# A long-convolution layer and a Mish MLP on one core: a reordered schedule, D's transfer first, and other V chunks

## The chip, the cores and the metric

The kernel runs on one core of a Trainium2 chip. A core has a matrix engine (TensorE, PE in the profile), which multiplies into PSUM, and four other engines: VectorE (DVE), ScalarE (ACT), GpSimd (POOL) and SyncE (SP), which here only issues DMAs. Each engine works through its own queue in order; semaphores tie them together. The metric is the device time of one execution in microseconds (us); lower is better.

## The reference

Two blocks, with a residual around each, on S = 2048 positions of D = 640 channels; the MLP has F = 1728 hidden units.

```python
def _A_ref(q, k, v, shift_k, ssm_k, ssm_D):
    k_shift = jnp.zeros_like(k)
    for t in range(4):                                   # short causal convolution of k
        k_shift = k_shift + k_pad[:, t:t + S, :] * shift_k[:, 3 - t][None, None, :]
    kv = k_shift * v
    y = irfft(rfft(kv, 2 * S) * rfft(ssm_k, 2 * S))[:S]  # long causal convolution, per channel
    y = y + kv * ssm_D[None, None, :]
    return q * y

def _B_ref(x, w1, b1, w2):
    h = einsum("bsd,df->bsf", x, w1) + b1
    act = h * tanh(softplus(h))                          # Mish
    return einsum("bsf,fd->bsd", act, w2)

x = A_q
h = x + _A_ref(_layernorm(x), A_k, A_v, A_shift_k, A_ssm_k, A_ssm_D)
return h + _B_ref(_layernorm(h), B_w1, B_b1, B_w2)
```

All inputs and the output are bfloat16.

## The kernel before

*The work.* The long convolution is a transform in two stages of matmuls, applied to the filter ("k" in the names) and to the product kv ("v"), a multiplication in the transformed domain, and two inverse stages. Channels come in five blocks of 128 (dc 0 to 4). Steps are tokens with a name, a block and a piece:

- `d_n0`..`d_n4` load the filter, 512 KB a block; `d_k0`..`3`, `d_v0`..`3`, `d_x0`..`3` load k, v and x (640 KB each), `d_g0`..`7` the table of the second stage (512 KB each), `d_cst` and `d_t2m`, `d_a12` other tables, `d_dr` the vector D, `d_w1*`, `d_w2*` the MLP's weights.
- D is folded into the filter: `dsel`, `dcol` (lines 273, 274) arrange it as a column for each block, and `dadd*` (line 364) adds it to the filter's first column. `k1pe*` transposes a filter block (line 370), and `k1ev*` (line 375) copies it out of PSUM. Block 0 is copied in two halves, `k1ev0` and `k1ev0b`.
- `s1kpe`, `s1kev`: first stage of the filter, 20 groups (lines 390, 391) and their copies; `s2kpe`, `s2kev`: second stage, 22 groups (line 416). A copy is line 256 on ACT and line 258 on DVE.
- `ktpe`, `ktev`, `ktsh`: k transposed (line 335), copied, shifted. `coef`, `wsh` (lines 303, 311) make the matrices of the short convolution; `kspe` (lines 351, 352) applies it and `kv` (line 356) multiplies with v on DVE.
- `s1v*`, `s2v*`: the two stages of kv. The second stage runs in chunks of channel blocks, `CHUNKS`; a group of a chunk may start when the first stage of all its blocks is copied out. `s2v0`, `s2v1`, `s2v2` are the chunks in their order.
- `sw*` (line 444): ten DMAs, two for each block, that swap the halves of the filter's transform within SBUF; `pr*` (line 455): 20 products on DVE; `i1pe`, `i1ev` (line 473): inverse first stage; `i2*`, `y` (line 525): inverse second stage and its copies.
- The first layer norm: `ln1_` (DVE statistics, lines 504, 505), `ln1p` (POOL, lines 509 to 511), `lnx` (ACT line 516 or POOL line 518). Then `wb`, `h` (lines 532, 534), the second norm `bn`, `pow`, `hc` (lines 538 to 544), and a transposition of each of 16 tiles of rows: the first two by PE (`trpe`, `trev`), the others by DMA (`tr`, line 557).
- The MLP: `m1pe` (lines 582, 589) with its activations `hb` (ACT, line 604), `m2pe` (lines 647, 655), `res` (line 672) and `d_out`. Rows come in units of 256, 256, 512, 512, 512.

*The order.* One list, `ORDER`, written out by hand, holds all 660 steps. The steps are emitted in this order, so each engine's queue is the list cut down to its own steps. `@n` names the PSUM tile that a PE group writes; there are four tiles, of two banks each, and a group waits until the earlier contents of its tile are copied out. `:a`, `:d`, `:p` pick ACT, DVE or POOL for a step that may run on more than one; without it the step runs on the first engine of its list. A DMA on SP's or ACT's queue takes one of eight semaphores in turn, and SP waits until the DMA eight places earlier has landed before it issues the next.

*Around the change.* ACT's queue begins with three DMAs, `d_cst`, `d_dr`, `d_sk`. SP's begins `d_n0 d_n1 d_n3 d_n4 d_k2 d_a12 d_k0 d_n2 d_k3 d_k1`. `dadd1` and `dadd2` run on DVE, the other three on POOL. The last steps before the MLP's matmuls are `wb0 h0 wb1 h1 bn0 bn1 wb3 hc0 h3 hc1` on DVE, and eleven `y` copies, `trev0` and `trev1` on ACT.

Of the kernel before, what the change touches and what calls it, by code (L numbers as in the profile page):

```python
# [30 lines left out]
s1kev2_1 ktpe1_3 ktpe4_0@2 wsh3 d_g0 ktev1 ktpe4_2 ktpe0_0@1 ktpe4_1 ktpe4_3 ktpe2_0@0 ktev4 ktpe3_0@3 ktpe2_2 ktpe3_3 d_g4 ktpe3_2 ktpe3_1 ktpe2_1
ktev3 s1kpe1_1@2 ktpe2_3 s1kev1_1 ktpe0_3 ktev2 ktpe0_1 ktsh3 d_g5 ktpe0_2 s1kpe3_0@3 ktsh1 s1kpe2_0@2 ktev0 ktsh4 s1kev3_0 kspe4_1@0 d_g3 ktsh2
s1kev2_0 ktsh0 kspe3_0@3 kv4_1 s1kpe2_3@1 s1kpe4_2@2 kv3_0 s1kev2_3 s1kpe4_0@0 s1kev4_2 s1kpe2_2@1 s1kev4_0:d kspe4_0@3 s1kev2_2 kspe0_0@2 kv4_0
s2kpe_96@0 s2kpe_30@1 kv0_0 s2kev_96 kspe1_0@3 s2kev_30 s2kpe_42@0 kv1_0 s2kpe_24@2 s2kev_42 kspe2_0@1 s2kev_24:d s2kpe_120@3 s2kpe_108@0 s2kev_120
kv2_0 kspe1_1@2 s2kev_108 s2kpe_12@3 kv1_1 d_x0 s2kpe_36@1 s2kev_12 d_x1 kspe0_1@0 s2kev_36:d s2kpe_90@2 s2kpe_48@3 s2kev_90 kv0_1 kspe2_1@1 s2kev_48
s2kpe_78@2 kv2_1 s1vpe4_1@0 s2kev_78 s2kpe_6@3 s1vev4_1 s2kpe_66@1 ln1_1 s2kpe_84@2 s2kev_66 kspe3_1@0 s2kev_84:d ln1p1 s2kev_6 s2kpe_0@1 kv3_1
s2kpe_60@2 s2kev_0 s1vpe2_0@3 s2kev_60 d_x2 s1vpe2_2@0 s1vev2_0:d s1vpe2_1@1 d_x3 s1vev2_2 s1vpe0_1@2 lnx1:p s1vev2_1:d s2kpe_102@3 s1vev0_1
s2kpe_72@0 s2kev_102:d s1vpe1_0@1 s2kev_72 s1vpe3_0@2 s1vev1_0 s1vpe0_2@3 s1vev3_0:d s1vpe1_3@0 s1vev0_2 s2kpe_126@1 ln1_0 s2kpe_114@2 s2kev_126
s1vpe2_3@3 s1vev1_3 s2kev_114:d s2kpe_54@1 ln1p0 s1vev2_3 s2kpe_18@0 s2kev_54:d s1vpe0_0@2 s2kev_18 s1vpe4_0@3 ln1_3 s1vpe3_2@1 s1vev0_0 sw2_1
s1vpe4_2@0 sw1_0 s1vev3_2:d s1vev4_0 ln1p3 s1vpe1_2@2 sw1_1 s1vev1_2 sw3_1 s1vpe1_1@3 s1vev4_2:d lnx3:p s1vpe3_3@1 sw4_1 s1vev1_1 s1vpe0_3@2  # L40
s1vev3_3:d lnx0:p sw3_0 s1vpe4_3@0 s1vev0_3 sw0_0 s1vpe3_1@3 ln1_2 sw2_0 s2v1pe_112@1 s1vev4_3 s2v1pe_96@2 sw0_1 s1vev3_1:d s2v1ev_112 ln1p2 sw4_0
s2v1pe_48@0 d_t2m s2v1ev_48 s2v1ev_96:d s2v1pe_32@1 lnx2:p s2v1pe_64@3 s2v1ev_32 s2v2pe_80@0 pr1_96 b1pe@2 s2v1ev_64 s2v1pe_80@1 pr1_32 s2v2ev_80
s2v1pe_0@3 s2v1ev_80:d s2v1ev_0 s2v1pe_16@0 s2v1ev_16 s2v2pe_32@3 pr1_64 s2v2pe_0@1 c_b1 s2v2ev_32 s2v2pe_48@0 pr1_0 s2v2pe_64@2 s2v2ev_48 pr2_64
i1pe1_0@3 s2v2ev_0 s2v2pe_112@0 pr2_96 s2v2ev_64 i1pe1_1@1 i1ev1_0 pr4_32 s2v2pe_16@2 s2v2ev_112 i1pe1_2@3 pr2_0 s2v2ev_16 pr2_32 s2v2pe_96@0 i1ev1_1
s2v0pe_0@2 pr3_0 i1ev1_2 i1pe2_3@1 s2v0ev_0 pr3_32 s2v0pe_64@3 s2v2ev_96 i1pe2_0@2 pr3_64 s2v0ev_64 s2v0pe_96@0 pr3_96 i1ev2_3 s2v0pe_32@3 pr4_0
i1ev2_0 i1pe2_1@1 d_w10 d_w11 s2v0ev_96 i1pe3_1@2 pr4_64 d_w12 i1ev2_1 d_w14 i1pe3_2@0 pr0_0 d_w13 s2v0ev_32 i1pe3_3@1 pr4_96 i1ev3_2 i1pe3_0@3
i1ev3_3 pr0_32 i1pe4_2@0 i1ev3_0 i1pe4_1@1 pr0_96 i1ev3_1 i1pe1_3@3 ln1_6 i1ev4_2 i1pe4_3@2 pr0_64 ln1p6 i1ev1_3 i1pe2_2@0 i1ev4_1 ln1_5 i1pe0_0@3
lnx6:p i1ev2_2 i1pe0_2@1 ln1_9 ln1p5 i1ev0_0 i1pe0_1@0 ln1_4 lnx5:p i1ev0_2 i1pe0_3@3 i1ev0_1:d ln1p4 i1ev4_3 i1pe4_0@1 ln1_7 i1ev0_3 ln1p9 d_w2b
i1ev4_0 d_w2c ln1_11 i2a1@0 d_w2a ln1p7 i2a0@2 i2b0 ln1_14 i2b1 i2pe9@3 y0 i2pe4@1 y1 wb0 i2a3@2 y9 h0 i2pe11@0 wb1 y4 i2b3 h1 i2a2@3 y11 bn0 i2b2
i2pe10@1 y2 i2pe5@0 y10 bn1 i2pe7@3 pow0 y3 i2pe6@1 y7 i2pe12@2 wb3 pow1 y6 hc0 h3 trpe0@3 y12 i2pe13@1 hc1 trev0:a wb2 trpe1@2 bn3 trev1:a i2pe8@3  # L50
y13 m1pe0_4@2 h2 pow3 y8 bn2 lnx9 ln1p11 m1pe0_2@1 hc3 y5 m1pe0_6@3 wb6 tr3 pow2 hb0_2 wb5 m1pe0_1@0 w2z lnx7 hc2 ln1_10 tr2 m1pe0_3@1 hb0_4 lnx11:p
hb0_6 h5 m1pe0_0@2 ln1p14 lnx4 ln1_15 hb0_3 m1pe0_5@3 h6 hb0_0 bn6 m1pe1_5@1 hb0_1 wb7 lnx14 pow6 m1pe1_4@2 bn5 ln1p15 hb1_5 m1pe1_1@0 hb1_4 hc6 h7
tr6 pow5 hb0_5 m1pe1_2@1 bn7 ln1p10 hb1_1 m1pe1_0@2 hc5 ln1_12 pow7 tr5 m1pe1_6@3 hb1_0 hc7 ln1p12 hb1_2 ln1_8 tr7 m1pe1_3@0 hb1_6 wb11 i2pe14@2 h11
hb1_3 wb4 i2pe15@1 wb9 lnx10 m2pe0@3 h4 h9 y14 bn4 lnx12 ln1_13 pow4 ln1p8 hc4 m2pe2@0 wb10 tr4 h10 ln1p13 lnx8 bn11 lnx15 bn10 pow11 y15 lnx13 wb8
pow10 hc11 m1pe2_3@2 res2 wb12 d_out2 h12 tr11 h8 m1pe2_2@1 wb14 res0 bn8 d_out0 m2pe1@0 bn9 pow8 wb13 pow9 hc8 hc10 wb15 tr10 h13 h14 m1pe2_4@3 hb2_3
hc9 tr8 bn13 hb2_2 tr9 h15 pow13 m1pe2_5@2 bn12 bn14 pow12 m1pe2_6@1 hb2_5 hc13 bn15 tr13 hb2_4 m2pe3@2 hc12 pow15 hb2_6 tr12 pow14 hc15 hc14 tr14
tr15 m1pe3_1@3 res3 res1 d_out3 d_out1 m1pe3_6@1 hb3_1 m1pe3_0@2 hb3_6 m1pe3_2@0 hb3_0 m1pe3_4@3 hb3_2 m1pe2_1@1 hb3_4 m1pe3_5@2 hb2_1 m1pe2_0@0 hb3_5
m1pe3_3@3 hb2_0 m2pe4@1 hb3_3 m2pe6@2 m2pe5@0 res6 res4 d_out6 d_out4 m2pe7@3 m1pe4_3@2 res7 res5 d_out5 d_out7 m1pe4_5@1 hb4_3 m1pe4_2@3 hb4_5
# [108 lines left out]
def kernel(  # L167
# [193 lines left out]

    k1_pes, k1_evs = [], []
    for b in range(NDC):
        dad = OP(f"dadd{b}", ["dve", "pool"], [d_n[b], o_dc], emit=lambda e, b=b: (nc.gpsimd if e == "pool" else nc.vector).tensor_tensor(raw_n[b][:, 0:1], raw_n[b][:, 0:1], dcol[:, b:b + 1], ALU.add))
# [12 lines left out]


# [339 lines left out]
```

## Time and profile before

| | us |
|---|---|
| median of 3 runs (228.49 to 228.54) | 228.52 |
| profiled execution, device time | 227.92 |
| its span, first to last instruction | 226.1 |
| PE busy in the span | 215.3 (95%) |
| DVE busy | 140.7 (62%) |
| ACT busy | 131.4 (58%) |
| POOL busy | 52.4 (23%) |

The profile records one execution. Times in it count from the first instruction. L364 is line 364 of the kernel. Busy time of PE includes waiting in its pipeline; a number in square brackets is the idle time of the engine ahead of an instruction, with what ended it. Shares over the whole span mix two very different halves, so the views below are cut into stretches. TensorE's clock was granted in full (1.00) throughout.

### The profile page before, as it was taken

Reading aid. Unit: us, or ns where it says so; the run is one execution under the profiler, and the core shown is the slowest. Engines: PE = TensorE matmul, PEld = TensorE weight load, DVE = VectorE, ACT = ScalarE, POOL = GpSimd, SP = SyncE. Lnnn points to the kernel's source line nnn. Section 1 sums busy time; section 2 is a strip of 40 time slices with the busy share of each in tenths; the row PEclk is TensorE's granted clock in tenths of the full one; section 3 lists DMA queues with packets and bytes.
Section 4 is the critical chain, followed back from the end, with each engine's and each line's share of the span. In section 5 each row is a group of like instructions: output and inputs, shape, how many; then the busy total and the mean of one; then the engine's idle time right before and its main releaser. Section 6 shows DMA issues by size and latency. Waiting matters only on the chain.

```text
span 226.1 us, 6202 instructions
## 1 busy us (share of the span) xinstructions
PE 215.3 (95%) x2690; PEld 157.5 (70%) x2690; DVE 140.7 (62%) x250; ACT 131.4 (58%) x181; POOL 52.4 (23%) x101
## 2 busy tenths in 40 slices
PE   7999999999979999999999999999999999999994
...
GB/s 206 371 421 415 418 343 33 210 232 97 414 412 206 167 259 4 185 192 33 29 77 38 62 58 89 137 12 3 0 0 58 29 32 0 3 29 46 58 53 48
DMA packets 19563, 30.98 MB, mean 137 GB/s; under 512 B 10704, under 2 KB 14928, under 8 KB 18768
## 3 DMA queue, kind: packets, MB, share of 16 engines
...
q14 instruction: 6, 0.05, 0.1%
...
HBM read 20.42 MB, written 2.62 MB: 102 GB/s over the span
## 4 chain that ended last, share of the span: by engine, by line
PE 67%; DMA 9%; DVE 9%; ACT 7%; SPq 3%; issue 3%; POOL 1%; DVEq 0%; ACTq 0%
PE ps L647 25%; PE ps L582 25%; DMA ks<-in_A_ssm_k_dram 6%; DVE ks L455 5%; PE ps L473 3%; ACT uv L256 3%; ACT ks L256 3%; SPq L444 3%; DMA ks<-ks 3%; PE ps L335 2%; PE ps L416 2%; PE ps L351 2%; PE ps L390 2%; PE ps L352 1%; PE ps L589 1%
## 5 line engine op out<-in xcount | busy, mean ns | idle before, releaser
L604 ACT ACTIVATE ks<-ps,b1s 128x512 bf16<-128x512 f32 (+1 forms) x69 | 36.2, 617 | 44.0 <-PE ps L582 35.8
L647 PE MATMUL ps<-ks 128*128 128x320 bf16 (+2 forms) x420 | 58.6, 299 | 0.0
L582 PE MATMUL ps<-G 128*128 128x512 bf16 (+1 forms) x325 | 57.6, 337 | 0.1
L672 DVE TENSOR_TENSOR rb<-ps,rb 128x640 bf16<-128x640 f32 x15 | 11.8, 820 | 68.4 <-PE ps L655 66.0
L647 PEld LDWEIGHTS <-ks 128*128 128x128 bf16 x420 | 40.6, 98 | 17.3 <-issue 1.3
L582 PEld LDWEIGHTS <-G 128*128 128x128 bf16 x325 | 31.3, 98 | 24.7 <-issue 1.6
L256 ACT CAST uv<-ps 128x1024 bf16<-128x1024 f32 x50 | 46.6, 1145 | 0.0
L256 ACT CAST ks<-ps 128x640 bf16<-128x640 f32 (+3 forms) x46 | 37.9, 898 | 10.1 <-PE ps L391 6.7
L455 DVE TENSOR_TENSOR ks<-ks,uv 128x2048 bf16<-128x2048 bf16 x20 | 23.0, 1221 | 0.8 <-DMA ks<-ks 0.6
L416 PEld LDWEIGHTS <-G 128*128 128x128 bf16 x512 | 20.9, 96 | 3.1 <-issue 2.5
L473 PE MATMUL ps<-a_t,ks 128*128 128x128 bf16 x320 | 19.2, 219 | 1.3 <-DVE ks L455 1.2
L473 PEld LDWEIGHTS <-ks 128*128 128x128 bf16 x320 | 18.2, 113 | 1.8 <-DVE ks L455 1.6
L509 POOL TENSOR_SCALAR ve<-mv 128x1 f32<-128x1 f32 x16 | 4.7, 294 | 48.2 <-DVE mv L505 47.3
L542 POOL TENSOR_TENSOR r<-ve,mhalf 128x1 f32<-128x1 f32 x16 | 10.2, 638 | 21.7 <-DVE ve L540 21.7
L416 PE MATMUL ps<-uv,G 128*128 128x64 bf16 (+1 forms) x384 | 12.9, 187 | 1.7 <-ACT uv L256 1.4
L538 DVE BATCH_NORM_STATS2 st<-rb 128x6 f32<-128x320 bf16 x32 | 14.1, 482 | 0.1
L258 DVE CAST ks<-ps 128x1024 bf16<-128x1024 f32 (+1 forms) x12 | 14.0, 1179 | 0.2
L504 DVE BATCH_NORM_STATS2 st<-rb 128x6 f32<-128x320 bf16 x32 | 13.9, 475 | 0.0
L356 DVE TENSOR_TENSOR ra<-ps,rb 128x1024 bf16<-128x1024 f32 x10 | 11.9, 1219 | 1.1 <-PE ps L352 0.7
L258 DVE CAST uv<-ps 128x1024 bf16<-128x1024 f32 x10 | 11.9, 1211 | 0.5 <-PE ps L391 0.2
L390 PE MATMUL ps<-cst,ks 128*64 128x128 bf16 x160 | 10.8, 220 | 0.9 <-DVE ks L258 0.5
L390 PE MATMUL ps<-cst,ra 128*64 128x128 bf16 x160 | 10.5, 219 | 0.8 <-ACT uv L256 0.5
...
## 6 DMA issues: line engine op xcount, KB each, us to landing
...
G<-tab_g SPq DMA_DIRECT2D x8, 512.0 KB, 11.4
...
```

The costliest lines, as they stand in the source:

```text
L256: nc.scalar.copy(o, i)
L258: nc.vector.tensor_copy(o, i)
L356: nc.vector.tensor_tensor(kv_w[:, m, :, 8 * h:8 * h + 8, :], p_.f32().rearrange("p (l t d) -> p d t l", l=4, t=8), raw_v[:, 8 * h:8 * h + ...
L390: nc.tensor.matmul(ps[0:64, dgl, :], lhs, mc, start=True, stop=True)
L416: nc.tensor.matmul(p_.f32()[:, o:o + n], g_v[:, f, :], src[:, :, f, :], start=True, stop=True)
L455: nc.vector.tensor_tensor(o, o, v, ALU.mult)
L473: nc.tensor.matmul(pz[:, dgl, :], KS[:, k, b, :, l], a12[:, k, :], start=k == 0, stop=k == 1)
L504: nc.vector.bn_stats(st1[:, t, hh, :], xt(t)[:, hh * 320:(hh + 1) * 320])
L538: nc.vector.bn_stats(st2[:, t, hh, :], xt(t)[:, hh * 320:(hh + 1) * 320])
L582: nc.tensor.matmul(ph[:, o:o + w], w1[:, dc, fc * P:fc * P + P], lt[:, dc, 0:w], start=dc == 0, stop=dc == NDC - 1)
L604: nc.scalar.activation(hb[:, fc, 0:n], p_.f32()[:, i * 512:i * 512 + n], ACT.Mish, bias=b1s[:, fc:fc + 1], scale=1.0)
L647: nc.tensor.matmul(p_.f32()[:, o:o + n], lhs, w2[:, k, cols:cols + n], start=fc == 0, stop=single and fc == 13)
```

## The change

It changes four things, and the order:

1. `d_dr` stands first on ACT's queue, ahead of `d_cst`.
2. The addition of D's column is a tensor and a scalar for each partition in place of two tensors. In the new order `dadd0` and `dadd1` run on DVE, the other three on POOL.
3. Both halves of the first copy, `k1ev0` and `k1ev0b`, run on DVE.
4. V's second stage takes blocks 0 and 1, then 2, then 3 and 4: chunks of 256, 128 and 256 channels in place of 128, 256, 256.
5. `ORDER` is new throughout. On SP's queue the five filter blocks come ahead of k, with one block of the second-stage table (`d_g3`) between them; `d_a12` moves behind the second swap, and `d_w11` ahead of the last. One of the five `ktev` copies (`ktev2`) goes to ACT. The second stage of V starts with chunk 0; the swaps start with blocks 0 and 1. In the MLP, `i2pe12` and `i2pe13` run behind the first two units' first layer, where `i2pe14` and `i2pe15` ran.

The diff, with the list cut to its first lines and those of V's second stage:

```diff
 ORDER = """
-d_cst wz idn d_n0 cz d_dr wm@0 small lane d_n1 d_sk d_n3 warm d_n4 d_k2 kz d_a12 dsel dcol d_k0 dadd0:p k1pe0@1 d_n2 dadd1 d_k3 k1pe1@2 k1ev0b:d
-k1ev0:a d_k1 s1kpe0_3@3 k1ev1 s1kpe0_0@0 s1kev0_3 dadd3:p d_v2 s1kpe0_2@1 s1kev0_0:d s1kpe0_1@2 k1pe3@3 s1kev0_1 dadd4:p d_v3 s1kev0_2:d cfpe@0
...
+d_dr wz idn d_n0 cz wm@0 small lane d_n1 d_cst d_sk d_n2 warm d_n3 d_n4 kz dsel d_g3 dcol dadd0 d_k0 k1pe0@1 d_k3 dadd1 k1pe1@2 d_k1 k1ev0 d_k2 k1ev0b
+s1kpe0_0@3 k1ev1 s1kpe0_3@0 s1kev0_0 dadd2:p d_v3 s1kpe0_1@1 s1kev0_3 s1kev0_1:d s1kpe0_2@2 dadd3:p d_g6 s1kpe1_0@3 s1kev0_2 k1pe2@0 dadd4:p d_g7
+s1kev1_0 cfpe@1 k1pe3@2 coef k1ev2:a s1kpe1_3@3 k1ev3 wsh0 k1pe4@1 d_v0 s1kev1_3 s1kpe2_0@0 k1ev4 s1kpe2_1@2 d_v2 s1kev2_0 wsh2 s1kpe3_0@3 s1kpe4_3@1
...
+s1vpe3_2@3 sw0_1 s1vev0_3 s1vpe2_1@2 sw3_1 s1vev1_0:d lnx0:p s1vev3_2 sw1_0 s1vpe4_2@1 ln1_3 sw4_1 ln1p1 s1vpe3_3@0 s1vev2_1 s2v0pe_80@3 sw3_0
+s1vev4_2 s1vev3_3:d sw2_1 s2v0pe_64@2 ln1p3 sw2_0 s2v0ev_64 s2v0pe_96@1 s2v0ev_80:d s2v0pe_48@0 lnx3:p s2v0ev_96 s2v0pe_16@2 pr0_64 lnx1:p s1vpe4_3@3
...
-CHUNKS = [[0], [1, 2], [3, 4]]
+CHUNKS = [[0, 1], [2], [3, 4]]
...
-        dad = OP(f"dadd{b}", ["dve", "pool"], [d_n[b], o_dc], emit=lambda e, b=b: (nc.gpsimd if e == "pool" else nc.vector).tensor_tensor(raw_n[b][:, 0:1], raw_n[b][:, 0:1], dcol[:, b:b + 1], ALU.add))
+        dad = OP(f"dadd{b}", ["dve", "pool"], [d_n[b], o_dc], emit=lambda e, b=b: (nc.gpsimd if e == "pool" else nc.vector).tensor_scalar(raw_n[b][:, 0:1], raw_n[b][:, 0:1], dcol[:, b:b + 1], None, ALU.add))
...
-            k1_evs[b].append(OP(f"k1ev{b}" + "b" * h, ["act", "dve"] if h else ["dve", "act"], [k1_pes[b], o_warm], uses=[p_],
+            k1_evs[b].append(OP(f"k1ev{b}" + "b" * h, ["dve"] if b in K1S else ["dve", "act"], [k1_pes[b], o_warm], uses=[p_],
```

More of the change, by code (lines that the diff above doesn't have):

```diff
@@ L31 @@
[L31 to L58, printed above, removed]
@@ new lines @@
+kspe3_1@2 ktev0 s1kpe4_2@3 s1kpe2_3@0 s1kev4_2 kv3_1 ktsh0 s1kpe3_3@1 s1kev2_3:d kspe4_0@3 s1kev3_3 kspe3_0@2 kv4_0 s2kpe_126@0 s2kpe_102@1
+s2kev_126:d s2kpe_18@3 s2kev_102 kv3_0 kspe2_0@0 s2kev_18 s2kpe_0@1 kv2_0 s2kpe_48@2 s2kev_0 kspe0_0@3 s2kev_48 s2kpe_24@0 kv0_0 kspe1_0@1 s2kev_24
+s2kpe_96@2 kv1_0 s2kpe_54@3 s2kev_96 kspe2_1@0 s2kev_54:d d_x0 s2kpe_36@1 d_x1 s2kpe_6@2 s2kev_36 kv2_1 kspe1_1@3 s2kev_6 s2kpe_66@1 kv1_1 s2kpe_84@0
+s2kev_66 kspe4_1@2 s2kev_84 s2kpe_120@3 kv4_1 s2kpe_42@1 s2kev_120 kspe0_1@0 ln1_2 s2kev_42 s2kpe_72@2 s1vpe2_3@3 s2kev_72 kv0_1 ln1p2 s2kpe_60@1
@@ new lines @@
+s2v2pe_80@1 s2v2ev_48 i1pe0_1@2 d_w11 s2v2ev_112 pr3_0 sw4_0 i1pe0_3@0 d_w10 i1ev0_1 pr2_32 i1pe1_2@3 d_x2 s2v2ev_80 d_w13 i1pe1_0@2 d_t2m pr2_64
+i1ev0_3 d_w12 i1pe0_2@1 d_w14 pr3_96 i1ev1_0 i1pe1_1@0 i1ev1_2 pr3_32 i1pe0_0@2 i1ev1_1 pr3_64 i1pe2_0@3 i1ev0_0 i1pe2_3@0 pr4_64 i1ev0_2 i1pe3_0@2
+pr4_96 i1ev2_3 i1pe3_2@1 i1ev3_0 pr4_32 i1pe2_2@0 i1ev3_2 pr4_0 i1pe3_1@2 i1ev2_0 i1pe2_1@1 ln1_8 i1ev2_2 i1pe3_3@3 ln1_5 i1ev3_1 ln1p8 i1pe4_3@0
+i1ev2_1 ln1_7 i1pe4_2@2 ln1p5 i1ev4_3 ln1_6 i1pe4_1@1 lnx5:p i1ev3_3 i1pe4_0@0 i1ev4_2:d ln1p7 i1ev4_1 i2a0@3 d_w2b ln1_11 b1pe@2 i1ev4_0 i2a1@1 d_w2c
@@ new lines @@
+ln1p6 d_w2a ln1_12 c_b1 i2b0 i2b1 i2pe10@0 y0 i2a2@2 y1 wb0 i2b2 i2pe7@3 h0 y10 wb1 i2pe15@1 y2 h1 i2pe9@0 y7 bn1 i2a3@2 y9 i2pe14@3 y15 bn0 i2b3 pow1
+i2pe6@0 y3 i2pe5@1 y6 wb2 i2pe11@2 pow0 hc1 y5 wb3 trpe1@0 y11 i2pe8@1 hc0 h3 trev1:a trpe0@2 bn3 trev0:a i2pe4@0 y14 m1pe0_4@2 h2 pow3 y8 bn2 lnx7
+ln1p12 m1pe0_6@3 m1pe0_3@1 hc3 hb0_6 ln1_4 hb0_4 tr3 pow2 m1pe0_0@3 hb0_3 lnx6:p hc2 wb7 lnx8 tr2 m1pe0_1@2 ln1p11 ln1_10 hb0_0 m1pe0_2@1 hb0_1 h7
+ln1p10 ln1_15 m1pe0_5@3 hb0_2 ln1p4 bn7 lnx12 m1pe1_3@2 hb0_5 wb5 ln1p15 m1pe1_0@1 ln1_13 hb1_3 lnx11 m1pe1_5@3 wb6 ln1p13 h6 y4 m1pe1_4@2 bn6 hb1_5
@@ new lines @@
+m1pe2_1@3 hb2_6 tr14 tr15 m1pe3_6@0 m1pe3_4@1 hb3_6 m1pe2_2@2 hb3_4 hb2_1 m1pe3_1@0 hb2_2 m1pe3_2@1 hb3_1 m1pe3_3@3 m1pe3_5@2 hb3_3 m1pe3_0@0 hb3_5
+hb3_2 m2pe4@3 hb3_0 m2pe6@2 m2pe5@1 res6 res4 d_out4 d_out6 m2pe7@0 m1pe4_6@2 res5 res7 d_out5 d_out7 m1pe4_5@3 hb4_6 m1pe4_3@1 m1pe4_1@0 hb4_3 hb4_5
+m1pe4_4@2 hb4_1 m1pe4_2@1 hb4_4 m1pe4_0@3 hb4_2 m2pe9@0 hb4_0 m2pe11@2 m2pe15a@1 res9 res11 d_out11 d_out9 m2pe8@3 res15a d_out15a m2pe10@0 m2pe12@2
+res8 res10 d_out8 d_out10 m2pe14@1 m2pe13@3 res12 res14 d_out12 d_out14 m2pe15b@0 res13 d_out13 res15b d_out15b
```

17 lines of the change are left out of this document (13 added, 4 removed).

## The prediction

> **What bounds the kernel now.** I read the page's first line, then busy time by stretch, then the chain of work that ended last, then the timelines of ScalarE (ACT) and VectorE (DVE) where that chain leaves TensorE, and last the groups, for durations.
>
> ```profile
> span 226.1 us, 6202 instructions
> ```
>
> Stretches (start:end, length, then busy us of each engine with its instruction count; the granted clock and the DMA share are at the end):
>
> ```profile
> core 0: us, PE busy (x) PEld busy (x) DVE busy (x) ACT busy (x) POOL busy (x), PEclk, DMA share, GB/s
> 6.90:16.80 9.90, 9.32 (x208) 8.36 (x208) 9.08 (x13) 7.82 (x7) 4.48 (x5) 1.00 1.02 411
> 16.80:32.80 16.00, 15.22 (x330) 14.29 (x331) 14.12 (x14) 8.72 (x9) 6.92 (x7) 1.00 1.01 412
> 32.80:54.00 21.20, 20.70 (x416) 18.99 (x415) 20.39 (x24) 19.91 (x24) 2.99 (x7) 1.00 0.41 134
> 54.00:62.00 8.00, 7.09 (x225) 6.55 (x220) 7.72 (x12) 8.00 (x10) 4.68 (x9) 1.00 0.83 343
> 62.00:94.00 32.00, 28.97 (x625) 27.43 (x622) 31.02 (x41) 31.65 (x36) 6.37 (x13) 1.00 0.57 197
> 102.00:118.00 16.00, 15.95 (x147) 13.60 (x146) 14.97 (x44) 15.02 (x36) 12.54 (x23) 1.00 0.28 42
> 118.00:223.20 105.20, 105.12 (x676) 61.54 (x674) 34.07 (x82) 30.90 (x50) 8.08 (x15) 1.00 0.14 40
> ```
>
> The kernel has two halves. From 102 us TensorE is full to the end: 15.95 of 16.00 and 105.12 of 105.20 us. Call this the train. Its start stands in the chain:
>
> ```profile
> 102.07 13.26 PE ps L582 x120
> ```
>
> The order changes no matmul's shape or number in the train, so a change there can only add gaps, and the 0.13 us of gaps are all it could remove. Up to 94 us the two engines that copy results out of PSUM are full, except ACT between 6.9 and 32.8 (9.36 us idle). So the time is decided by two things: how much work ACT and DVE have in their queues before the train can start, and how long they stand idle meanwhile. The chain of the first 24 us shows what holds them:
>
> ```profile
> 5.76 9.52 DMA ks<-in_A_ssm_k_dram
> ...
> 15.30 0.05 DVE ks L364
> 15.35 1.38 issue
> 16.73 2.35 DVE ks L258 x2
> ...
> 19.77 4.20 PE ps L335 x64
> ```
>
> The last filter block lands at 5.76 + 9.52 = 15.28 us, because it is issued eleventh; DVE's addition to it takes until 16.73; two DVE copies follow; only then do the transposes of K begin, at 19.77. ACT, meanwhile:
>
> ```profile
> 17.76 3.07 ACT L256 CAST ks<-ps 128x1024 bf16<-128x1024 f32 x3 [1.40 <-PE ps L391]
> 24.58 1.01 ACT L256 CAST ks<-ps 128x1024 bf16<-128x1024 f32 x1 [3.76 <-PE ps L391]
> 26.29 1.93 ACT L256 CAST ks<-ps 128x1024 bf16<-128x1024 f32 x2 [0.69 <-DVE uv L258]
> 28.98 2.84 ACT L256 CAST ks<-ps 128x1024 bf16<-128x1024 f32 x3 [0.77 <-PE ps L391]
> 32.86 0.96 ACT L256 CAST ks<-ps 128x960 bf16<-128x960 f32 x1 [1.03 <-DVE ra L356]
> ```
>
> Brackets are idle time ahead: 1.40 us behind the late block, 3.76 us while sixteen K transpose groups stand on PE and all their five copies are DVE's.
>
> **The change, part by part.** First the work in the two queues up to DVE's second normalised tile and ACT's second transposed copy, which release the train. I counted the tokens of both orders and priced those that differ. ACT's copies, DVE's copies, its two additions (shortest/median/longest in ns), the small first copy, and the statistics:
>
> ```profile
> L256 ACT CAST uv<-ps x50: 1012/1138/1272, 42.0 to 92.5; 128x1024 bf16<-128x1024 f32 x50
> ...
> L256 ACT CAST ks<-ps x32: 485/1012/1057, 8.6 to 94.6; 128x960 bf16<-128x960 f32 x15, 128x1024 bf16<-128x1024 f32 x14, 128x640 bf16<-128x640 f32 x2, 128x320 bf16<-128x320 f32 x1
> L256 ACT COPY ks<-ps x2: 1012/1438/1865, 7.6 to 11.4; 128x1024 bf16<-128x1024 bf16 x1, 128x2048 bf16<-128x2048 bf16 x1
> ```
>
> ```profile
> L258 DVE CAST ks<-ps x12: 1104/1184/1225, 9.4 to 52.6; 128x1024 bf16<-128x1024 f32 x6, 128x960 bf16<-128x960 f32 x6
> L258 DVE CAST uv<-ps x10: 1171/1216/1225, 45.7 to 90.7; 128x1024 bf16<-128x1024 f32 x10
> L258 DVE COPY uv<-ps x5: 1215/1225/1225, 21.0 to 26.2; 128x2048 bf16<-128x2048 bf16 x5
> ```
>
> ```profile
> L364 DVE TENSOR_TENSOR ks<-ks,dcol x2: 162/839/1516, 6.8 to 15.3; 128x1 bf16<-128x1 bf16 x2
> ```
>
> ```profile
> 6.89 0.68 DVE L258 COPY ks<-ps 128x1024 bf16<-128x1024 bf16 x1
> ```
>
> ```profile
> L504 DVE BATCH_NORM_STATS2 st<-rb x32: 440/476/496, 41.8 to 121.6; 128x6 f32<-128x320 bf16 x32
> ```
>
> DVE: one K copy fewer (five to four) -1.23; two additions at 162 ns in place of one at 162 and one at 1516, -1.35; one more half copy, since the first copy is its own alone, +0.68; six K second-stage copies become four and the small one (about 1.14 each, between the row's shortest and its median, and 0.5), -1.78; one more inverse copy +1.22; one statistics pair fewer -0.95. Sum -3.4 us. ACT: the half copy -1.01; one K copy at 1.87; fifteen and the small second-stage copy become seventeen, +2.0 -0.49; one inverse copy fewer -1.14. Sum +1.2 us. Both together -2.2 us; with both engines full, half of it reaches the end: -1.1 us.
>
> The long addition: the group says that one of two equal additions took 1516 ns, and it ends at 16.82, when POOL's second product ends (12.71 + half of 8.14 = 16.78):
>
> ```profile
> 12.71 8.14 POOL L311 TENSOR_TENSOR rw<-cst,coef 128x1120 bf16<-128x1120 bf16 x4 [2.77 <-DVE coef L303]
> ```
>
> DVE waited for POOL, not for data. In the new order DVE's two additions come near 6.8 us, before any product, and the other three are POOL's own. So column plus scalar should cost what column plus column did, 0.16; its bounds are 0.16 and 1.52 each, from the same row, and I take the low end, because POOL is free then. The Trainium skill ("SBUF — State Buffer", section Who interferes with whom) says that a DVE instruction with two inputs in SBUF contends with a GpSimd one that reads SBUF; by that rule, the row agrees. It also speaks against the change, whose spectral products (two SBUF inputs, L455) start earlier, beside POOL's two normalisations of
>
> ```profile
> L518 POOL TENSOR_SCALAR ra<-rb,r,nmr 128x640 bf16<-128x640 bf16 x7 | 6.1, 870 | 3.1 <-PE ps L391 2.7
> ```
>
> At most one of these, 0.87 us, lies beside DVE's first product. Were DVE held that long, half would reach the end: 0.4 us, which I leave in the range.
>
> Next the idle time, by walking the new queues with these durations.
>
> ```profile
> 7.61 1.01 ACT L256 COPY ks<-ps 128x1024 bf16<-128x1024 bf16 x1 [3.63 <-DVE ks L258]
> 8.60 1.01 ACT L256 CAST ks<-ps 128x1024 bf16<-128x1024 f32 x1
> ```
>
> *Start.* The first DVE copy still starts at 6.89, behind the second filter block (0.16 us after that block's addition); D's earlier arrival frees only an addition that waits for the first block anyway, so I price it at nothing. The table cst now lands behind the first block; it is used just ahead of ACT's copy at 8.60, and were it late, ACT and PE would shift by as much. ACT loses its half copy and starts at 8.60, so 1.0 us more idle; DVE's second half is done at 8.2 instead of ACT's 8.62.
> *Filter blocks.* The queue moves 411 GB/s, 1.27 us for each 512 KB. All five blocks now come ahead of K, the last near 11 us; a block of the G table passes K, which moves K's last quarter 1.1 us back, to 18.4 to 19.5 (K is 640 KB a quarter, 1.6 us). Its first transposes are eighth in the queue, at 19.9, so this costs nothing unless it lands 0.5 us later still. The 1.40 us gap goes. New is 1.3 us on DVE at 10.7: the small matmul for the shift coefficients stands behind the third block's transposes on PE.
> *K transposes.* The five filter copies are done at 16.0 instead of 19.1, the K transposes start at 18.2 instead of 19.77, and ACT, which now has one of the five copies, waits 2.35 us instead of 3.76.
> *Second stage of K.* All twenty first-stage copies are done at 29.4, and ACT's first second-stage copy starts at 30.4 instead of 32.86, with DVE one product behind. V lands before its use, by 0.3 us at the nearest.
> ACT's idle time up to 94 goes from 11.0 us (9.36, 1.29 and 0.35 in the stretches) to 8.3; DVE's from 4.8 to 6.0. That is -1.5 us, or -0.75 at the end, and with the work -1.85.
>
> *Middle.* Walked on, the last copy of K's second stage ends at 50.9 (54.2), and the ten half-swaps, which wait for it, start 3.3 us earlier. Swaps of the first two blocks now come first, as their V chunk does: the first product is due at 57.7 and its swap at 57.3. One W1 load stands ahead of the last swap on SP's queue and waits for a V matmul near 69; that swap then lands at 73.5, and its product is due at 80. The chunk sizes 256, 128, 256 need the same 384 matmuls and 20 copies. The first output copy starts at 91.7 against 94.0: -2.3 us. From there to the train both orders have ten DVE instructions and thirteen ACT copies on the path, so the lead stays. Bookkeeping says -1.85 and the walk -2.3; I take -2.1.
>
> *Train.* No term. It would take a tile's transfer or a PSUM tile coming late; the nearest is a transposed tile with 0.2 us to spare, as before.
>
> The profiled execution took 227.92 us around its span of 226.1, so 1.8 us lie outside; it becomes 225.8. The median of the runs, 228.52, is 0.6 above it: forecast 226.4.
>
> **The rivals.** *The gain is swallowed in the middle.* From 32.8 to 54 PE is busy 20.70 of 21.20 us, as full as the copying engines. If PE there is the bound, an early start gains only what PE's own queue gains, and the copies that ACT and DVE saved go into idle time. For it: that fullness. Against it: busy PE time contains waiting in its pipeline, and ACT and DVE have no gaps to speak of either. It would leave the end of this stage 0 to 0.9 us early: 227.6 to 228.5.
>
> *ACT starves the train (slower).* The fullest stretch for ACT after 94 is 102 to 118: 0.98 us idle.
>
> ```profile
> L604 ACT ACTIVATE ks<-ps,b1s 128x256 bf16<-128x256 f32 x27 | 10.7, 534 | 1.0 <-PE ps L582 0.9
> ...
> L516 ACT ACTIVATE ra<-rb,nmr,r 128x640 bf16<-128x640 bf16 x5 | 4.8, 961 | 0.0
> ```
>
> The new order has five normalisations (0.96 us) there instead of four, which uses up that idle time, and an unread output tile keeps one of the four PSUM tiles until its copy, behind fourteen other steps of ACT. Eleven matmul groups then rotate through three tiles. My walk frees each tile 0.4 us or more before PE wants it. Past that point every normalisation standing before a needed activation costs PE up to 0.96; three of the five make 2.9 us: 226.4 + 2.9 = 229.3, slower by 0.8. For it: no slack is left. Against it: only the first rotation is that tight, and the two activations of a tile overlap.
>
> *The change does less than it says*: the V stream and the products are bound by swaps, whose start depends only on K's second stage. That is within the first rival.
>
> **How the numbers follow.** A measurement of this kernel can tell 0.2%, 0.46 us, from no change. Forecast 0.62, its own range 225.3 to 227.6, all faster. Swallowed 0.19: 0.08 faster, 0.09 the same, 0.02 slower. Starved 0.19: 0.02 the same, 0.17 slower. Together 0.70, 0.11, 0.19. The range reaches from 225.3 (the walk's 2.3 and 0.9 more, if the copying engines lose half of their left idle time) to 229.0, which leaves out the worst of the last rival and a little below.
>
> **What would show it.** In the new profile: no 1.5 us addition on DVE; the third link of the early chain not a filter block; K's transposes from about 18.2; ACT's first 960-wide copy near 30.4; swaps from 51; TensorE's full stretch from just under 100 and 121 us long. I am wrong if that stretch starts at 101 or later, or if ACT's activations make PE wait inside it.

## The result, and the profile after

The changed kernel takes 227.43 us (median; its runs lie between 227.22 and 227.81) against 228.52 us for the kernel before in the same session: ratio 0.9950, 95% interval 0.9927 to 0.9972. That is 1.1 us faster; 2.1 us were forecast. A second set of runs gave 227.45 us and 0.9969 (0.9954 to 0.9983), against 228.28 us for the kernel before in that session. The profiled execution took 227.22 us around this span:

```profile
span 225.2 us, 6200 instructions
```

Busy time by stretch, with the stretches that the prediction cut (the last one ends just behind this trace's last matmul):

```profile
core 0: us, PE busy (x) PEld busy (x) DVE busy (x) ACT busy (x) POOL busy (x), PEclk, DMA share, GB/s
6.90:16.80 9.90, 9.76 (x235) 9.30 (x237) 7.52 (x12) 7.87 (x8) 4.64 (x5) 1.00 1.02 416
16.80:32.80 16.00, 15.52 (x326) 14.52 (x321) 14.16 (x14) 10.92 (x12) 7.36 (x8) 1.00 1.00 410
32.80:54.00 21.20, 20.78 (x441) 19.03 (x440) 19.72 (x25) 20.27 (x23) 2.96 (x7) 1.00 0.38 126
54.00:62.00 8.00, 6.65 (x189) 5.78 (x184) 6.80 (x10) 8.00 (x10) 4.68 (x9) 1.00 1.00 397
62.00:94.00 32.00, 29.20 (x626) 27.52 (x626) 31.05 (x41) 31.33 (x36) 5.03 (x13) 1.00 0.66 242
102.00:118.00 16.00, 16.00 (x148) 13.56 (x147) 15.45 (x44) 15.89 (x36) 13.48 (x27) 1.00 0.15 33
118.00:222.30 104.30, 103.91 (x663) 60.87 (x666) 33.75 (x82) 28.18 (x46) 8.75 (x16) 1.00 0.14 41
```

Two things are to be seen. In 102 to 118, ACT is busy 15.89 of 16.00 us and PE misses nothing: the rival in which ACT starves the train did not happen. And up to 94 us the idle time went the other way on the two copying engines. ACT's is 8.71 us (2.03, 5.08, 0.93, 0 and 0.67 by stretch; before: 11.0), DVE's is 7.85 (2.38, 1.84, 1.48, 1.20, 0.95; before: 4.8).

The chain that ended last, its first part and the start of the train:

```profile
1.46 5.30 DMA ks<-in_A_ssm_k_dram
6.81 1.21 PE ps L370 x16
...
18.44 4.14 PE ps L335 x64
...
53.63 5.80 DMA ks<-ks
59.65 1.05 issue
60.70 1.22 DVE uv L258
...
101.17 14.35 PE ps L582 x130
```

The late filter block and DVE's long addition are gone from it; an early swap within SBUF (ks<-ks) that lands at 59.43 us has come in (in the kernel before the chain runs through the last swap, which lands at 70.43). The train starts at 101.17 instead of 102.07, 0.9 us earlier. From there to the end of its last matmul, at 222.23, are 121.06 us; before it was 121.05.

The additions of D by shape (us in all, mean ns; idle before):

```profile
L364 POOL TENSOR_SCALAR ks<-ks,dcol 128x1 bf16<-128x1 bf16 x3 | 0.9, 291 | 6.6 <-DMA ks<-in_A_ssm_k_dram 6.6
L364 DVE TENSOR_SCALAR ks<-ks,dcol 128x1 bf16<-128x1 bf16 x2 | 0.4, 216 | 3.2 <-DMA ks<-in_A_ssm_k_dram 3.2
```

ACT's timeline, and DVE's in the first 20 us and around the first product:

```profile
15.38 3.76 ACT L256 CAST ks<-ps 128x1024 bf16<-128x1024 f32 x4 [0.30 <-PE ps L391]
21.60 1.86 ACT L256 COPY uv<-ps 128x2048 bf16<-128x2048 bf16 x1 [2.46 <-PE ps L335]
...
30.82 5.74 ACT L256 CAST ks<-ps 128x960 bf16<-128x960 f32 x6 [1.27 <-PE ps L416]
```

```profile
9.52 1.22 DVE L258 CAST ks<-ps 128x1024 bf16<-128x1024 f32 x1 [0.20 <-PE ps L391]
11.94 1.01 DVE L303 CAST coef<-ps 32x80 bf16<-32x80 f32 x4 [1.20 <-PE ps L298]
13.15 1.23 DVE L258 COPY ks<-ps 128x2048 bf16<-128x2048 bf16 x1 [0.20 <-PE ps L370]
14.80 1.22 DVE L258 COPY ks<-ps 128x2048 bf16<-128x2048 bf16 x1 [0.43 <-PE ps L370]
16.34 3.49 DVE L258 CAST ks<-ps 128x1024 bf16<-128x1024 f32 x3 [0.31 <-PE ps L391]
...
59.55 1.23 DVE L455 TENSOR_TENSOR ks<-ks,uv 128x2048 bf16<-128x2048 bf16 x1 [1.16 <-DMA ks<-ks]
```

DVE waits before four of the seven copies that it begins in the first stretch, 0.20, 0.20, 0.43 and 0.31 us, beside the foreseen wait (1.20, where 1.3 was forecast), and it waits 1.16 us for a swap before the first product.

Executions differ in when the second filter block lands (6.26 to 7.50 us in the thirteen profiled executions of this study); DVE's second addition follows at once, and much of what is behind it shifts. So the table counts from that addition. "Lead" is how much shorter the stretch from the addition to the train is than before. The count is a help and no exact measure. For the changed kernel, profiled twice with nearly the same landing, it differs by 0.02 us. But the kernel with the early block and the same with POOL exchanged have the same steps up to the train, and their counts differ by 0.44, with additions 1.25 us apart. So leads are compared to some tenths of a microsecond only, unless the additions start at about the same time.

| kernel | second addition | train starts | between | lead | last matmul ends | median, us | ratio to before |
|---|---|---|---|---|---|---|---|
| before | 6.82 | 102.07 | 95.25 | 0 | 223.12 | 228.52 | 1 |
| after | 6.79 | 101.17 | 94.38 | 0.87 | 222.23 | 227.43 | 0.9950 |
| after, again | 6.89 | 101.29 | 94.40 | 0.85 | 222.35 | 227.45 | 0.9969 |
| before + form | 7.29 | 101.26 | 93.97 | 1.28 | 222.31 | 227.15 | 0.9937 |
| before + early block | 6.35 | 100.52 | 94.17 | 1.08 | 222.43 | 227.64 | 0.9974 |
| the same, POOL exchanged | 7.60 | 101.33 | 93.73 | 1.52 | 222.51 | 227.17 | 0.9943 |
| the same, D first | 7.05 | 101.17 | 94.12 | 1.13 | 222.34 | 227.16 | 0.9955 |
| after, swaps exchanged | 6.89 | 100.77 | 93.88 | 1.37 | 221.82 | 226.66 | 0.9931 |
| the same, late POOL tile | 6.81 | 100.66 | 93.85 | 1.40 | 221.72 | 226.62 | 0.9927 |
| the same, table block late | 6.63 | 100.36 | 93.73 | 1.52 | 221.42 | 226.87 | 0.9940 |
| after, column form | 6.70 | 101.64 | 94.94 | 0.31 | 222.70 | 227.76 | 0.9976 |
| after, half copy on ACT | 6.83 | 101.32 | 94.49 | 0.76 | 222.38 | 227.99 | 0.9970 |
| after, D second | 7.41 | 101.86 | 94.45 | 0.80 | 222.92 | 227.57 | 0.9960 |

The medians come from four sessions, in which the kernel before took 228.25 to 228.52 us; each ratio is to the kernel before in the same session. The ratios' intervals are about 0.002 to each side, so the runs alone tell apart what lies 0.5 us or more from each other; smaller steps are read from the traces, which are one execution of each kernel.

### The profile page after: what moved, and what is told of

The parts are those of the page before. It is cut to its first block, busy times and chain, and to the rows that moved or that the text cites. A ratio compares the mean times of both kernels' runs of the same rounds, so it can differ in the third digit from the quotient of the medians.

```text
span 225.2 us, 6200 instructions
## 1 busy us (share of the span) xinstructions
PE 214.5 (95%) x2684; PEld 157.5 (70%) x2690; DVE 137.9 (61%) x250; ACT 131.8 (59%) x180; POOL 51.4 (23%) x102
## 4 chain that ended last, share of the span: by engine, by line
PE 69%; DVE 9%; ACT 8%; issue 6%; DMA 5%; POOL 1%; SPq 1%; DVEq 0%; ACTq 0%
PE ps L647 26%; PE ps L582 25%; ACT uv L256 5%; PE ps L473 4%; PE ps L390 3%; ACT ks L256 3%; DVE ra L356 3%; DVE ks L455 3%; DMA ks<-ks 3%; PE ps L335 2%; DMA ks<-in_A_ssm_k_dram 2%; PE ps L370 2%; DVE uv L258 2%; PE ps L589 1%; PE ps L655 1%
## 5 line engine op out<-in xcount | busy, mean ns | idle before, releaser
L256 ACT CAST uv<-ps 128x1024 bf16<-128x1024 f32 x49 | 45.5, 1089 | 0.5 <-ACT uv L256 0.4
L256 ACT CAST ks<-ps 128x960 bf16<-128x960 f32 (+2 forms) x47 | 39.0, 910 | 8.6 <-PE ps L391 6.1
L473 PE MATMUL ps<-a_t,ks 128*128 128x128 bf16 x320 | 18.2, 219 | 0.8 <-DVE ks L455 0.8
L416 PE MATMUL ps<-uv,G 128*128 128x64 bf16 (+1 forms) x384 | 12.4, 187 | 2.5 <-DVE uv L258 1.9
L509 POOL TENSOR_SCALAR ve<-mv 128x1 f32<-128x1 f32 x16 | 4.2, 260 | 43.2 <-DVE mv L505 42.1
L258 DVE CAST uv<-ps 128x1024 bf16<-128x1024 f32 x11 | 13.0, 1202 | 0.2 <-ACT uv L256 0.2
L258 DVE CAST ks<-ps 128x1024 bf16<-128x1024 f32 (+2 forms) x11 | 12.1, 1126 | 1.6 <-PE ps L391 1.6
L416 PE MATMUL ps<-ks,G 128*128 128x160 bf16 x128 | 11.2, 230 | 0.6 <-DVE ra L356 0.2
L390 PE MATMUL ps<-cst,ra 128*64 128x128 bf16 x160 | 11.0, 219 | 0.5 <-ACT uv L256 0.4
```

The source lines that it names most:

```text
L256: nc.scalar.copy(o, i)
L258: nc.vector.tensor_copy(o, i)
L390: nc.tensor.matmul(ps[0:64, dgl, :], lhs, mc, start=True, stop=True)
L416: nc.tensor.matmul(p_.f32()[:, o:o + n], g_v[:, f, :], src[:, :, f, :], start=True, stop=True)
L473: nc.tensor.matmul(pz[:, dgl, :], KS[:, k, b, :, l], a12[:, k, :], start=k == 0, stop=k == 1)
```

## The experiments

### The form of the addition alone

```diff
-tensor_tensor(raw_n[b][:, 0:1], raw_n[b][:, 0:1], dcol[:, b:b + 1], ALU.add)
+tensor_scalar(raw_n[b][:, 0:1], raw_n[b][:, 0:1], dcol[:, b:b + 1], None, ALU.add)
```

This is in the kernel before, with nothing else changed.

> The kernel before, with the addition of D's column written as a tensor and a scalar, all else as it was: DVE's second addition still stands beside POOL's products at 15.3 us. Port theory (DVE waited because its addition had two inputs in SBUF while POOL read SBUF): with one tensor input it takes about 0.2 us instead of 1.52, the fifth filter block is copied out 0.6 to 1.3 us earlier, and the time falls by 0.3 to 0.7 us. Rival (DVE waits for POOL whatever the form is, or waits for something else that ends at 16.8): the addition still takes 1.5 us and the time stays within 0.2 us of before.

Measured: 227.15 us, ratio 0.9937 (0.9910 to 0.9965). DVE's timeline in the kernel before, then DVE's, POOL's and ACT's here:

```profile
13.99 1.22 DVE L258 CAST ks<-ps 128x1024 bf16<-128x1024 f32 x1
15.30 1.52 DVE L364 TENSOR_TENSOR ks<-ks,dcol 128x1 bf16<-128x1 bf16 x1
```

```profile
14.51 1.23 DVE L258 CAST ks<-ps 128x1024 bf16<-128x1024 f32 x1
15.65 0.21 DVE L364 TENSOR_SCALAR ks<-ks,dcol 128x1 bf16<-128x1 bf16 x1
```

```profile
13.22 8.15 POOL L311 TENSOR_TENSOR rw<-cst,coef 128x1120 bf16<-128x1120 bf16 x4 [2.88 <-DVE coef L303]
```

```profile
17.56 2.84 ACT L256 CAST ks<-ps 128x1024 bf16<-128x1024 f32 x3 [0.68 <-PE ps L391]
```

The addition stands inside POOL's four products, as in the kernel before, and takes 0.21 us instead of 1.52. Nothing else was changed, so the 1.3 us were DVE's wait for POOL, and the form of the operands ended it. The Trainium skill ("SBUF — State Buffer", section Who interferes with whom) says that a DVE instruction with two inputs in SBUF contends with a GpSimd one that reads SBUF, and one with at most one such input, outside certain faster modes, doesn't; by that rule, both rows agree, if the scalar for each partition is not counted as an input. The median falls by 1.10 us, more than the 0.3 to 0.7 expected, and the lead is 1.28 us: about all that the stall had cost, and no less than the whole change brings.

The rows also say what the late filter block cost. In the kernel before it lands at 15.28 us, and DVE is busy until 15.21, so DVE hardly waited for it. Here it lands no earlier (15.41), and ACT's gap behind it shrinks from 1.40 to 0.68 us all the same.

### The late filter block alone

```diff
-... d_n1 d_sk d_n3 warm d_n4 ... k1pe0@1 d_n2 dadd1 ... coef ... d_g7 dadd2 wsh1
+... d_n1 d_sk d_n2 d_n3 warm d_n4 ... k1pe0@1 dadd1 ... s1kev0_3 dadd2:p dadd3:p ... d_g7 wsh1
```

> The kernel before, with the last filter block issued ahead of the blocks 3 and 4 and its addition (still two tensors) on POOL ahead of POOL's other two. Start theory (the gain of the change is made in the first 20 us, by the filter block that came late and by the addition that stood on DVE): the long addition goes, ACT's gap of 1.40 us before 17.76 shrinks below 0.6, the transposes of K start 0.8 to 1.4 us before 19.77, and the time falls by 0.5 to 1.1 us, most of what the whole change gained. Rival (the gain lies in how the later copies are shared out between ACT and DVE): the time falls by less than 0.3 us although the transposes start earlier.

The last block's addition, `dadd2`, also goes from DVE to POOL, still in the column form, so this edit takes away both the late block and DVE's long addition.

Measured: 227.64 us, ratio 0.9974 (0.9956 to 0.9992). ACT's gap is 0.68 us, as with the form alone (below 0.6 was expected), and the lead of 1.08 is no larger than with the form alone: these runs show no gain from the early block beyond the stall. The train starts 1.55 us earlier than before, but 7.95 us into it there is a gap. The chain and PE's timeline:

```profile
105.01 3.33 DMA G<-rw
108.33 0.14 issue
108.47 3.54 PE ps L582 x31
```

```profile
108.47 6.16 PE L582 MATMUL ps<-G 128*128 128x256 bf16 x55 [0.69 <-DMA G<-rw]
```

PE waits for the second of the tiles that a DMA transposes. In the kernel before and with the form alone this matmul comes 7.09 us after the train's start, so 0.86 us of the lead is lost here. The tile took 3.33 us from issue to landing. The DMA traffic in that time, and in the same time of the kernel before, where it took 2.38 us:

```profile
q1 hardware_dynamic: 675, 0.16, 21.4%
q14 instruction: 1, 0.01, 1.2%
...
G<-rw SPq DMA_TRANSPOSE x1, 3.3
```

```profile
q1 hardware_dynamic: 672, 0.16, 36.4%
...
G<-rw SPq DMA_TRANSPOSE x1, 2.4
```

One packet with instructions comes in. It starts at 106.94 and takes 0.65 us on its DMA engine, while the tile's 640 data packets run from 106.18 to 106.92; the last of the small packets that end the transfer ends with it, at 107.6, and the landing is seen at 108.33. In the kernel before a like packet starts at 106.85, and the tile's data follow only from 107.73 on. So the earlier train brought its tile to the time of the fetch.

### The same with POOL's steps exchanged

```diff
-... bn2 lnx9 ln1p11 m1pe0_2@1 hc3 y5 m1pe0_6@3 wb6 tr3 pow2 hb0_2
+... bn2 lnx9 m1pe0_2@1 hc3 y5 m1pe0_6@3 wb6 tr3 pow2 ln1p11 hb0_2
```

> The kernel before with the late filter block early, as in the experiment whose train had a gap, and POOL's second normalised tile done after the small power step that the second transposed tile waits for. Theory (that transposed tile came 0.9 us late because an instruction fetch lay on one DMA engine among its packets, 3.3 us from issue to landing in place of 2.4): the tile is issued about 0.8 us earlier, lands at 106.6 to 107.6 and the train, from 100.5, runs without a gap to about 221.6; span 224.6, time 0.8 us below that experiment's (226.8). Rival (the gap comes from a PSUM tile or from ScalarE's copies, as the rival of the prediction has it): the gap of 0.7 to 0.9 us stays 8 us into the train, and the time is 227.6.

Measured: 227.17 us, ratio 0.9943 (0.9923 to 0.9962). The tile is issued 3.82 us into the train instead of 4.49, and again takes 3.3 us, with an instruction packet of 0.34 us (at 107.01) in its time:

```profile
q14 instruction: 1, 0.01, 0.6%
...
G<-rw SPq DMA_TRANSPOSE x1, 3.3
```

PE's timeline, one row for the first 97 matmuls of the train, marks no gap at that place:

```profile
101.33 10.87 PE L582 MATMUL ps<-G 128*128 128x256 bf16 x97
```

The matmul that waited now comes 7.22 us into the train: 0.73 us of the 0.86 are back for a tile issued 0.67 us earlier. So the tile's transfer made the gap, and no PSUM tile did. The tile is as late with a packet of 0.34 us as with one of 0.65, so the packet's own time does not set the delay; how it delays the landing is open. The median fell by 0.5 us (0.7 by the ratios, each to its own session), less than the 0.8 expected; in the profiled execution the second filter block landed 1.24 us later than in the one before it (7.50 against 6.26).

### The order of the first swaps

```diff
-... sw0_0 ... sw1_1 ... d_a12 ... sw0_1 ... sw3_1 ... sw1_0
+... sw0_0 ... sw0_1 ... d_a12 ... sw1_1 ... sw1_0 ... sw3_1
```

> The changed kernel, with the swaps of blocks 0 and 1 in the order 0_0, 0_1, 1_1, 1_0, and 3_1 behind them; nothing else moves. Swap theory (DVE stood idle before its first product, 58.4 to 59.55 us, for the fourth transfer of the stream): the first product starts at 58.4 to 58.7, DVE's idle time there goes, ACT's gap of 0.4 us near 75 goes with it, and the time falls by 0.3 to 0.6 us. Port theory (DVE waited for POOL's two normalisations, which ended at 59.45): the swap lands by 58.1 and the first product still starts or ends about when it did (60.8), and the time does not move. Covered theory (DVE has time to spare, ACT sets the end): the product starts earlier and the time moves by less than 0.15 us.

Measured: 226.66 us, ratio 0.9931 (0.9906 to 0.9956). In the changed kernel the two halves that the first product needs are the first swap and the third, behind a swap and a table: they landed at 54.69 and 59.43 us. Now the second lands at 58.17. DVE's timeline:

```profile
58.60 1.22 DVE L455 TENSOR_TENSOR ks<-ks,uv 128x2048 bf16<-128x2048 bf16 x1
```

The first product starts at 58.60 instead of 59.55 with no wait ahead of it, and the train at 100.77 instead of 101.17. Of 0.95 us (1.05 counted from the second addition), 0.40 (0.50) reach the train. The second profile of the changed kernel, with its addition at 6.89 as here, gives 0.52.

### The same without POOL's tile beside the product

```diff
-... pr0_64 lnx1:p s1vpe4_3@3 ...
+... pr0_64 s1vpe4_3@3 ... ln1p8 lnx1:p i1pe4_3@0
```

> The changed kernel with the swaps in that order, and the second of POOL's two normalisations moved from beside DVE's first product to a place behind POOL's next statistics, some 28 us later. Port theory: only now does the first product start at 58.4 to 58.7, and this kernel is 0.3 us or more faster than the one with the swaps alone. Swap theory: the same as the one with the swaps alone, within 0.15 us.

Measured: 226.62 us, ratio 0.9927 (0.9903 to 0.9950); first product at 58.50. POOL's timeline, two normalised tiles in the changed kernel, two with the swaps exchanged, one here:

```profile
57.73 1.72 POOL L518 TENSOR_SCALAR ra<-rb,r,nmr 128x640 bf16<-128x640 bf16 x2
```

```profile
57.84 2.73 POOL L518 TENSOR_SCALAR ra<-rb,r,nmr 128x640 bf16<-128x640 bf16 x2
```

```profile
57.74 0.87 POOL L518 TENSOR_SCALAR ra<-rb,r,nmr 128x640 bf16<-128x640 bf16 x1
```

Beside DVE's first product the second tile takes 1.88 us instead of 0.87, and the product 1.22 as ever. POOL waited for DVE, not DVE for POOL, and nobody waits for that tile. So the 0.4 us that the prediction kept in its range for a held product were not needed.

### The column form in the new order

```diff
-tensor_scalar(raw_n[b][:, 0:1], raw_n[b][:, 0:1], dcol[:, b:b + 1], None, ALU.add)
+tensor_tensor(raw_n[b][:, 0:1], raw_n[b][:, 0:1], dcol[:, b:b + 1], ALU.add)
```

> The changed kernel with its five additions as column plus column again. Theory (the form only matters for an addition of VectorE that lies beside one of POOL's products): in the new order no addition does, so the additions cost 0.16 us on VectorE as in the kernel before, K's transposes start at 18.4 and the full stretch of TensorE at 101.2, and the time is that of the change within 0.2 us (227.2 to 227.6). Rival (the form is cheaper by itself, wherever it stands): the transposes and all behind them come 0.2 us or more later, and the time is 0.4 us or more above the change's.

Measured: 227.76 us, ratio 0.9976 (0.9957 to 0.9995). The additions by shape:

```profile
L364 DVE TENSOR_TENSOR ks<-ks,dcol 128x1 bf16<-128x1 bf16 x2 | 0.3, 164 | 3.2 <-DMA ks<-in_A_ssm_k_dram 3.2
```

They take 0.16 us, since none lies beside a product of POOL's, and k's transposes start at 18.28 (18.37 with the scalar form). The scalar form by itself is not cheaper; it is 0.05 us dearer. But the median lies 0.3 us above the changed kernel's, a little outside the 227.2 to 227.6 expected, and in the trace the train came 0.47 us later. There the reason is another one. PE's timeline:

```profile
18.28 1.95 PE L335 MATMUL ps<-ident,ra 128*128 128x128 bf16 x28
20.53 1.65 PE L335 MATMUL ps<-ident,ra 128*128 128x128 bf16 x23 [0.31 <-DMA ra<-in_A_k_dram]
```

K's last quarter landed at 20.48 us here (19.43 in the changed kernel), and the transposes waited. That is the reservation of the prediction, "unless it lands 0.5 us later still", come true in one execution. Whether it explains the median as well is not shown; the two ratios' intervals overlap.

### The half copy on ScalarE

```diff
-OP(f"k1ev{b}" + "b" * h, ["dve"] if b in K1S else ["dve", "act"], ...
+OP(f"k1ev{b}" + "b" * h, ["act", "dve"] if h else ["dve", "act"], ...
```

> The changed kernel with the second half of the first copy on ScalarE again. By the work in the queues ScalarE gains 1.01 us and VectorE loses 0.68, half of the difference at the end: +0.15 us. By the walk of the queues ScalarE's first result copy is held from 8.63 to about 8.7, and VectorE is free 0.7 us earlier at a place where it waits for the first transposes anyway: 0.0 to +0.2 us, K's transposes at 18.4 to 18.6. Rival (the small copy is what cost the lead): K's transposes start before 18.2 and the time falls by 0.3 us or more.

Measured: 227.99 us, ratio 0.9970 (0.9951 to 0.9989). The median is 0.5 us above the changed kernel's, but its runs lie between 227.29 and 228.30, and the ratio is nearly that of the changed kernel's second set of runs (0.9969). In the trace, an execution of 227.37 us, ACT's first result copy starts at 8.69, k's transposes at 18.52, and the train comes 0.11 us later, counted from the second addition. By the trace this part of the change is worth about 0.1 us; the runs can't tell it from nothing.

### The constant table first, D second

```diff
-d_dr wz idn d_n0 cz wm@0 small lane d_n1 d_cst d_sk d_n2
+d_cst wz idn d_n0 cz wm@0 small lane d_n1 d_dr d_sk d_n2
```

> The changed kernel with the constant table's transfer first and D's after the second filter block, as in the kernel before. Theory (as the prediction has it, D's early arrival only frees additions that wait for the filter blocks anyway): the first product copy still starts at 6.9, K's transposes at 18.4, the time is the change's within 0.2 us. Rival (D's early arrival is part of the gain): D lands at 5.5 to 6.7, both additions and the copy behind them start up to 0.6 us later, and the time rises by 0.3 to 0.6 us.

Measured: 227.57 us, ratio 0.9960 (0.9944 to 0.9976). Here the second filter block landed at 7.38 and all came 0.6 us late; counted from the second addition, the train is 0.07 us later than in the changed kernel, which is less than such counts can tell. Whether D's place had made the block late was asked of the next run.

### D first in the kernel before with its early block

```diff
-d_cst wz idn d_n0 cz d_dr wm@0 small lane d_n1 d_sk d_n2
+d_dr wz idn d_n0 cz wm@0 small lane d_n1 d_cst d_sk d_n2
```

> The kernel before with the late filter block early and POOL's two steps exchanged, and D's transfer first with the constant table behind the second filter block. In the profiled executions so far VectorE's second addition started at 6.35, 6.82, 7.29, 7.41 and 7.60 us with the table first and at 6.70 to 6.83 with D first. If D's place steadies and advances that block: addition at 6.7 to 6.9, train at 100.4 to 100.7, median 0.2 to 0.4 us below the same kernel without this (226.8 to 227.0). Rival (chance of the execution): same median, 227.0 to 227.3.

Measured: 227.16 us against 227.17 without it. The addition started at 7.05 us, neither as late as 7.60 nor where it was expected (6.7 to 6.9). The second transposed tile has an instruction packet in its time here too (0.31 us, 1.86 us after its issue) and takes 3.25 us. No gain from D's place is shown. With D first the second filter block landed at 6.61 to 6.96 us in eight profiled executions, with the table first at 6.26 to 7.50 in five; the range is narrower, but the times don't show it.

### K's last quarter earlier, and the changed kernel again

```diff
-... kz dsel d_g3 dcol dadd0 d_k0 ... k1ev0 d_k2 k1ev0b
+... kz dsel dcol dadd0 d_k0 ... k1ev0 d_k2 d_g3 k1ev0b
```

This is on top of the exchanged swaps and the late POOL tile.

> The changed kernel with the five first swaps in the other order and the late POOL tile moved, as in the two experiments before, and the block of the G table sent behind K's last quarter instead of ahead of K. Theory (K's last quarter lands with little to spare: it held the transposes by 0.5 us in the run with column plus column, where it landed at 20.5): it now lands at 18.2 to 18.7, no transpose waits for it, the median falls by 0 to 0.3 us against the same kernel without this (226.3 to 226.6). Rival (the quarter is never late but by chance): same, 226.6 to 226.8.

> The changed kernel once more, to be compared in one call with the other two and to see how far one execution's landings differ from another's. Theory: the lead of TensorE's full stretch, counted from VectorE's second addition, is again 94.4 us, plus 0.4 to 0.5 where K's last quarter lands at 20.4 or later; median 227.2 to 227.7. Rival (the lead differs from execution to execution by more than these two landings): the count comes out over 0.3 us off.

Measured: 226.87 us, ratio 0.9940 (0.9920 to 0.9960), and 227.45 us for the changed kernel. The quarter landed at 18.07 and the count to the train fell by 0.12 us, but the median did not fall (226.3 to 226.8 were expected by one theory or the other): that K's last quarter usually holds this kernel is not shown. The changed kernel's count was 94.40 again, 0.02 off.

## Why the prediction was right, and its gain twice too large

*Faster, for half of the reason named first.* DVE's long addition held the chain, and either edit that removes it, the form or the early block, by itself brings the train forward by about as much as the whole change, or more. The new order also removes it without the form (column form: no addition over 0.2 us, transposes at 18.28). That the last filter block was late, which the prediction put beside the addition, cost nothing that these runs show: it landed 0.07 us after DVE came free.

*The train has no term.* Right: 121.06 us against 121.05, no gap, ACT busy 15.89 of 16.00. "The nearest is a transposed tile with 0.2 us to spare" was the right place to look at: in the kernel before with its early block it did come late, by 0.86 us, with an instruction packet in its time that the prediction did not count.

*The walk: 2.3 us promised, 0.87 found.* By its own signs: k's transposes at 18.37 (18.2 foreseen), ACT's first 960-wide copy at 30.82 (30.4), end of K's second stage 51.60 (50.9), first swap 51.67 (51), first product 59.55 (57.7), first output copy 92.99 (91.7), train 101.17 (99.8). The prediction said that it is wrong if the train starts at 101 or later. In that it was wrong. The time stayed in its range, but the range ran from 225.3 to 229.0 us, so this says little for the walk. Two of its steps failed:

1. *Start, to Second stage of K.* The walk left almost no time for handing a tile from engine to engine. The trace has 0.20, 0.20, 0.43 and 0.31 us ahead of DVE's copies in the first stretch alone. By 30.8 us the trace was 0.4 us behind the walk and by 51.6 us 0.7. The rows show the waits; no run removed them, so that they made this share is read, not tested.
2. *Middle.* "The first product is due at 57.7 and its swap at 57.3" fits swaps that land 1.2 us one behind the other, as the first four do in the kernel before (57.93 to 61.59). In the changed kernel the first landed 3.0 us after its issue, the second 3.3 us behind it, and only then did they come 1.2 to 1.4 us apart; the needed one was third and landed at 59.43. Exchanging the swaps gave back 0.50 of the 1.4 us that were missing.

With 0.7 us lost before the swaps and 0.50 by their order, about 0.2 of the 1.4 us stay unassigned. Against the kernel before, K's second stage ends 2.56 us earlier (51.60 against 54.16), but the first output copy is only 1.02 us earlier (92.99 against 94.01). The walk had 3.3 and 2.3 there: it knew that the middle gives back some of the lead, and had this 0.5 us too small.

*The bookkeeping: -1.85 promised.* The term that was mis-sized is DVE's idle time: 6.0 us foreseen, 7.85 found, of which 1.14 are the waits of the first stretch and 1.16 the wait for the swap; ACT's 8.71 against 8.3 was near. With the measured idle times (-2.29 and +3.08) in place of -2.7 and +1.2, and the forecast work of -2.2, the sum is -1.4, half of it -0.7, close to the 0.87. But the rule "half of it reaches the end" is not borne out by itself: the addition was priced at 1.35 us of DVE's work, 0.7 at the end, and the form alone brought 1.10 by the medians and 1.28 by the count. This stall stood in the chain, and nearly all of it reached the end.

*The rivals.* "Swallowed in the middle" would have left the end of K's second stage 0 to 0.9 us early; it is 2.56 us early, so a full PE does not bound that stage as this rival has it. From ACT's first 960-wide copy to that end the walk lost 0.3 us more; whether PE, busy for 20.78 of 21.20 us, had a part in that is not shown.

*The other parts* are worth little: by the traces the half copy about 0.1 us, D's place 0.07, both less than the runs can tell. The chunks of 256, 128 and 256 channels were not tried by themselves, since the order is written around them. As a whole, the new order without its swaps exchanged is 0.3 us behind the form alone by the medians and 0.4 by the lead (0.87 against 1.28), no more than runs and counts can tell. With them exchanged it has the best medians of the study, 226.62 and 226.66 us, 0.5 us below the form alone in the same session.
